# A two-stage fused kernel: first load moved to another issuer as f32, late rows re-laid on every fourth partition and gathered in two transfers, first tiles added singly

## The chip, the cores and the metric

The kernel runs on one core of one Trainium2 chip. The views show five engines of a core, each with its own instructions: TensorE (PE, with PEld its weight loads), VectorE (DVE), ScalarE (ACT), GpSimd (POOL) and SyncE (SP), and 16 DMA engines. The metric is the device time of one execution in microseconds (us), as a median of several runs; the profile of one execution gives a span that is about 1.8 us shorter than that run's time. "PEclk" in a view is the clock granted to TensorE, 1.00 being full. All runs quoted are in the same state ("fast").

Two measures appear below beside the time. One is a view of the profile, copied as it stands. The other is worked out from the single packet records of the DMA engines in the trace; those tables stand in ordinary fences, and I say how each number was formed. Packet times are counted from the same zero as the views.

## The reference, cut to what matters

```python
def phi(x): return np.where(x > 0, x, np.exp(x) - 1.0) + 1.0

# stage 1: linear attention, q, k, v are [8 batches, 8 heads, 576, 64] f32
q_p, k_p = phi(q), phi(k)
kv  = einsum('bhsd,bhse->bhde', k_p, v);  z = sum(k_p, axis=2)
x   = einsum('bhsd,bhde->bhse', q_p, kv) / (einsum('bhsd,bhd->bhs', q_p, z) + 1e-6)
x   = x as [8, 576, 512]                                      # heads side by side

# stage 2: spectral mixing, w_r and w_i are [64 modes, 512, 512] f32
X = rfft(x, axis=1)[:, :64]
Y = X @ (w_r + 1j * w_i), mode by mode                        # complex, 64 of 289 modes kept
y = irfft(Y, n=576, axis=1)
u = x + y
return u + maximum(u @ w_ch, 0.0)                             # [8, 576, 512] f32
```

The weights dominate: 64 modes times 2 times 1 MB is 134 MB, q, k and v are 28 MB, the output is 9.4 MB.

## The kernel before

All loads of q, k, v and weights go out from GpSimd and are cast on the way (f32 in memory, f16 or bf16 on the core: one batch's q is 1.18 MB in memory and 576 KB in the profile's list of DMA issues). The weights stream through a ring of buffers for nearly the whole run. What can be done before the last weight lands is done before: attention rows, the inverse transform of modes 0 to 31 (to 55 for batches 0 and 1), and the products of all modes to 55 with `w_ch`. What is left for after the last weight is a tail: the modes 56 to 63 ("late modes") are transposed, multiplied with `w_ch`, sent to the partitions where the inverse transform wants them, and then 36 tiles of 128 rows are finished in 18 pairs, rectified and stored.

The head. GpSimd issues q, k and v of batch 0; SyncE at the same time issues two small constants:

```python
    nc.sync.dma_start(out=id16, in_=id16_dr.ap())          # 128x128 f16
    nc.sync.dma_start(out=fwd_sb, in_=fwd_dr.ap())         # 160 KB f16
    ...
    def load(b):
        for nm, src in (("q", q), ("k", k), ("v", v)):
            t = sA.tile([128, NHP, NJ * Dh], F16, tag=f"{nm}16", bufs=2, name=f"{nm}16_{b}")
            pin(nc.gpsimd.dma_start(out=t, in_=src[b].rearrange(...)))
            raw[nm, b] = t

    def features(b):                       # phi(x) = min(exp(x), max(x, 0) + 1)
        ...                                # tensor_scalar on raw, tensor_tensor min
```

The last mode. The last weight half comes in two parts, three quarters and one; before it PE is kept busy by six filler matmuls (`keep_warm`), then multiplies in the two parts:

```python
        product(1, wr, range(NDC))
        keep_warm(FILL[kk][0])                              # FILL[63] = (6,)
        product(0, wi, range(3))
        product(0, wi, range(3, NDC))
        nc.vector.tensor_copy(out=YT[:, :, kk, :], in_=y_last)
```

The gather. `last` holds the 128 rows of the late modes (8 modes x real and imaginary x 8 batches), in two planes: Y itself and Y times `w_ch`. `YZ[b]` holds for batch b the rows of modes 32 to 63, twice (partitions 0 to 63 and 64 to 127); rows 48 to 63 of each half are the late ones and come from `last`, by one 32 KB transfer for each batch and half. Two of the sixteen are not needed:

```python
    for b in (2, 3, 0, 1, 4, 5, 6, 7):
        for h in range(1 if b < N_LEAD else 2):
            nc.gpsimd.dma_start(out=YZ[b][64 * h + 48 : 64 * h + 64, :, :], in_=last[b::B, :, :])
```

Tile pairs 0 to 3 (batches 0 and 1) need no gather: they multiply `last` directly. Pair 4 is the first to need it. Tiles 0 and 1 are stored singly (256 KB each), later tiles in pairs (512 KB), all from SyncE:

```python
    store(0, 1)
    relu(0, 1);  rectified(1);  channels(2)
    add_inverse(0, 0, (1,))
    ...                                                     # add tile 1
    store(1, 1)
    channels(3);  rectified(2)
    finish(1)                                               # tiles 2 and 3 as a pair
    ...
```

## Time and profile before

| | before |
|---|---|
| time, median of 3 runs | 429.22 us (429.17 to 429.39) |
| span of the profiled run | 427.4 us |
| DMA load queue, share of the span | 99.0% |
| last weight landed (its DMA's semaphore complete) | about 394.3 us |
| first store issued | 398.08 us |

The page's table of DMA queues (packets, MB, share of 16 engines' span) and the shares by engine of the chain of waits that ended last, for the kernel before:

```profile
q0 software_dynamic: 32256, 82.26, 99.0%
...
DMA 73%; PE 12%; DVE 6%; issue 5%; POOL 1%; ACT 1%; DVEq 0%; POOLq 0%
```

The run is bound by one queue of casting loads that never stops. A change that gives time back must make this queue start sooner, or shorten what comes after its last byte. So two stretches matter.

The windows view of the kernel before: the stretch in us, its length, busy time and instructions of PE, PEld, DVE, ACT and POOL, then PEclk, the DMA share and the GB/s moved. A casting load is counted by its 16-bit bytes (82.26 MB on the load queue, 0.46 MB of it gathers, for about 164 MB in memory), so 205 GB/s of it read 410 GB/s from memory; a store or an f32 load counts in full. The share can exceed 1.

```profile
2.00:3.00 1.00, 0.00 (x0) 0.00 (x0) 0.00 (x0) 0.22 (x2) 1.00 (x3) 1.00 0.66 164
3.00:4.00 1.00, 0.00 (x0) 0.00 (x0) 0.00 (x0) 0.00 (x0) 1.00 (x2) 1.00 0.79 77
9.00:10.00 1.00, 0.00 (x0) 0.00 (x0) 0.00 (x0) 1.00 (x2) 0.00 (x0) 1.00 1.21 205
...
397.00:398.00 1.00, 1.00 (x6) 0.48 (x5) 0.89 (x2) 0.59 (x2) 0.77 (x2) 1.00 0.00 0
399.00:400.00 1.00, 1.00 (x7) 0.49 (x6) 0.40 (x2) 0.85 (x2) 1.00 (x3) 1.00 0.86 297
401.00:402.00 1.00, 1.00 (x6) 0.46 (x6) 1.00 (x1) 0.75 (x3) 1.00 (x3) 1.00 0.47 160
403.00:404.00 1.00, 1.00 (x6) 0.16 (x5) 1.00 (x2) 0.98 (x3) 0.92 (x2) 1.00 0.90 285
405.00:406.00 1.00, 1.00 (x10) 0.26 (x6) 0.97 (x2) 0.77 (x2) 0.00 (x0) 1.00 0.90 307
```

The timeline of the kernel before (start, length, engine, line, operation, number of instructions, and in brackets the idle time before and what ended it), head and tail:

```profile
0.74 0.34 SPq L85 DMA_DIRECT2D id<-ident  x1
1.26 0.90 POOL L164 DMA_DIRECT2D q<-in_q_dram  x1 [0.82 <-POOLq L820]
8.15 2.22 ACT L182 ACTIVATE qe<-q 128x1152 f16<-128x1152 f16 x2 [5.92 <-DMA q<-in_q_dram]
11.05 2.22 ACT L182 ACTIVATE ke<-k 128x1152 f16<-128x1152 f16 x2 [0.68 <-DMA k<-in_k_dram]
...
394.64 0.22 DVE L402 CAST YT<-y_last 128x64 f16<-128x64 f32 x1 [2.69 <-PE y_last L391]
397.23 6.69 POOL L771 DMA_DIRECT2D YZ<-last  x14 [17.79 <-DVE last L765]
398.08 9.41 SPq L671 DMA_DIRECT2D out_dram<-x_main  x8
```

Issuing the first q load takes GpSimd 0.90 us, and q is used only at 8.15 us. The 14 gathers take GpSimd 6.69 us, from 397.23 to 403.9. The cast of `y_last` at 394.64 follows directly on the products of the last weight, so I use it below as the tail's start.

### The profile page before, as it was taken

Reading aid. Unit: us, or ns where it says so; the run is one execution under the profiler, and the core shown is the slowest. Engines: PE = TensorE matmul, PEld = TensorE weight load, DVE = VectorE, ACT = ScalarE, POOL = GpSimd, SP = SyncE. Lnnn points to the kernel's source line nnn. Section 1 sums busy time; section 2 is a strip of 40 time slices with the busy share of each in tenths; the row PEclk is TensorE's granted clock in tenths of the full one; section 3 lists DMA queues with packets and bytes.
Section 4 is the critical chain, followed back from the end, with each engine's and each line's share of the span. In section 5 each row is a group of like instructions: output and inputs, shape, how many; then the busy total and the mean of one; then the engine's idle time right before and its main releaser. Section 6 shows DMA issues by size and latency. Waiting matters only on the chain.

```text
span 427.4 us, 6617 instructions
## 1 busy us (share of the span) xinstructions
PE 285.4 (67%) x2692; PEld 158.9 (37%) x2692; DVE 212.1 (50%) x432; ACT 153.7 (36%) x240; POOL 95.6 (22%) x173
## 2 busy tenths in 40 slices
PE   0357777788119765655333697777788788999991
PEld 0346655564003433333111333433333344374320
DVE  0699998956003755556200433443354344421893
ACT  3588666640102100000000244444353353431781
POOL 4233223212201322112112122122122122010600
PEclk9996666656557755555555569999898899799996
DMA  8999999999999999999999999999999999996698
GB/s 146 207 208 209 209 210 209 211 214 214 218 212 214 213 214 213 215 212 214 213 213 214 213 214 212 214 214 214 214 213 214 214 214 212 213 213 135 211 404 313
DMA packets 35854, 92.46 MB, mean 216 GB/s; under 512 B 3216, under 2 KB 16400, under 8 KB 35824
## 3 DMA queue, kind: packets, MB, share of 16 engines
q0 software_dynamic: 32256, 82.26, 99.0%
q1 hardware_dynamic: 3568, 9.78, 6.0%
q8 instruction: 21, 0.34, 0.3%
q14 instruction: 9, 0.07, 0.0%
HBM read 163.93 MB, written 9.44 MB: 406 GB/s over the span
## 4 chain that ended last, share of the span: by engine, by line
DMA 73%; PE 12%; DVE 6%; issue 5%; POOL 1%; ACT 1%; DVEq 0%; POOLq 0%
DMA wr<-in_moe_w_r_dram 48%; DMA wi<-in_moe_w_i_dram 13%; DMA pick_sb<-row_pick 4%; DMA q<-in_q_dram 4%; DMA k<-in_k_dram 4%; PE P L349 3%; PE acc L616 3%; DVE x L267 2%; PE acc L655 2%; PE z L579 1%; PE zb L606 1%; PE eps L557 1%; PE zb L605 1%; DVE qe L195 1%; ACT ke L182 1%
## 5 line engine op out<-in xcount | busy, mean ns | idle before, releaser
L349 PE MATMUL P<-wi,xt_c 128*32 128x512 bf16 x252 | 37.8, 536 | 39.7 <-DMA wi<-in_moe_w_i_dram 39.7
L360 ACT CAST ys<-P 128x512 f16<-128x512 f32 x31 | 18.2, 586 | 125.3 <-PE P L349 125.3
L110 POOL DMA_DIRECT2D wr<-in_moe_w_r_dram x64 | 34.0, 532 | 124.4 <-PE P L349 102.2
L110 POOL DMA_DIRECT2D wi<-in_moe_w_i_dram x65 | 34.5, 531 | 117.7 <-PE P L349 82.8
L358 DVE CAST ys<-P 128x512 f16<-128x512 f32 x32 | 22.1, 691 | 72.3 <-PE P L349 72.2
L349 PEld LDWEIGHTS <-xt_c 128*32 128x32 bf16 x504 | 28.9, 155 | 76.3 <-issue 65.2
L349 PE MATMUL P<-wr,xt_c 128*32 128x512 bf16 x252 | 37.5, 532 | 23.0 <-DMA wr<-in_moe_w_r_dram 20.8
L538 DVE TENSOR_TENSOR x_main<-ya,x_main 128x512 f32<-128x512 f32 x32 | 22.1, 691 | 39.7 <-PE ya L534 39.6
L557 PE MATMUL eps<-wch,xTw 128*128 128x512 f16 x144 | 41.3, 415 | 0.0
L146 PEld LDWEIGHTS <-qT 64*128 64x128 f16 (+1 forms) x640 | 23.3, 126 | 41.1 <-issue 20.7
L365 PE MATMUL yt<-pick_sb,ys 128*128 128x16 f16 x252 | 16.5, 175 | 25.5 <-DMA pick_sb<-row_pick 15.1
L540 ACT CAST x16w<-x_main 128x512 f16<-128x512 f32 x32 | 19.8, 618 | 34.7 <-DVE x_main L538 34.7
L565 ACT CAST E<-eps 128x512 f16<-128x512 f32 (+1 forms) x40 | 21.3, 543 | 26.6 <-PE eps L557 26.6
L146 PE MATMUL num<-kv,qT 64*128 64x65 f16 (+1 forms) x320 | 13.5, 223 | 22.5 <-ACT kv L242 18.7
L365 PEld LDWEIGHTS <-ys 128*128 128x128 f16 x252 | 12.2, 102 | 40.5 <-issue 17.8
L182 ACT ACTIVATE qe<-q 128x1152 f16<-128x1152 f16 x16 | 17.7, 1155 | 22.7 <-DMA q<-in_q_dram 22.7
L211 PE MATMUL qTp<-id,qe 128*128 128x128 f16 x144 | 16.8, 312 | 12.4 <-DVE qe L195 12.0
L267 DVE TENSOR_TENSOR x<-num,rd 128x512 f16<-128x512 f32 x32 | 22.1, 692 | 1.1
L146 PE MATMUL nw<-kv,qT 64*128 64x65 f16 (+1 forms) x320 | 19.6, 236 | 1.1 <-DVE x_tail L508 0.9
L211 PEld LDWEIGHTS <-qe 128*128 128x128 f16 x144 | 14.7, 147 | 13.2 <-DVE qe L195 12.0
L182 ACT ACTIVATE ke<-k 128x1152 f16<-128x1152 f16 x16 | 17.7, 1155 | 4.9 <-DMA k<-in_k_dram 4.9
L665 ACT ACTIVATE acc<-acc 128x512 f32<-128x512 f32 x34 | 18.1, 581 | 2.3 <-PE acc L616 1.7
(101 smaller groups left out, 451.8 us busy)
## 6 DMA issues: line engine op xcount, KB each, us to landing
wr<-in_moe_w_r_dram POOLq DMA_DIRECT2D x64, 512.0 KB, 18.8
wi<-in_moe_w_i_dram POOLq DMA_DIRECT2D x63, 512.0 KB, 18.9
out_dram<-x_main SPq DMA_DIRECT2D x14, 512.0 KB, 5.8
q<-in_q_dram POOLq DMA_DIRECT2D x8, 576.0 KB, 13.1
k<-in_k_dram POOLq DMA_DIRECT2D x8, 576.0 KB, 14.5
v<-in_v_dram POOLq DMA_DIRECT2D x8, 576.0 KB, 16.7
out_dram<-x_main SPq DMA_DIRECT2D x4, 256.0 KB, 3.6
out_dram<-x_tail SPq DMA_DIRECT2D x2, 512.0 KB, 5.3
```

Source lines behind the costliest of these rows:

```text
L110: tc.keep_in_program_order(nc.gpsimd.dma_start(out=w[:, dcs], in_=rows_of[:, dcs, :]))
L146: mm = nc.tensor.matmul(num[hpo][orow, c0 : c0 + 65], qT[rows, hpp, h2, cols], kv_sb[rows, hpp, h2, :])
L182: pin(nc.scalar.activation(out=ev[:, c], in_=heads(nm, b)[:, c], func=AF.Exp))
L211: nc.tensor.transpose(qT_ps[:, j].rearrange("p t r -> p (t r)"), phi["q", b][:, hpp, j].rearrange("p o d -> p (o d)"), id16,)
L267: nc.vector.tensor_tensor(out=dst.rearrange("p (o c d) -> p o c d", o=2, c=4), in0=nv[:, :, :, 0:64], in1=rden.unsqueeze(3).broadcast_to([ ...
L349: nc.tensor.matmul(P[dc * 32 : dc * 32 + 32, :], xt_cols(dc, t, kk), w[:, dc, :], start=(t == 1), stop=(t == 0), tile_position=(0, dc * 32),)
L358: fixed(nc.vector.tensor_copy(out=st, in_=P))
L365: nc.tensor.matmul(yt_ps[:, ec, kk % 8, :], st[:, ec * 128 : ec * 128 + 128], pick_sb)
L538: pin(nc.vector.tensor_tensor(out=x, in0=acc, in1=x, op=ALU.add))
L540: pin(nc.scalar.copy(out=x16w[t], in_=x))
L557: nc.tensor.matmul(e_ps, xT[:, c, :], wch16[:, c, :], start=(c == 0), stop=(c == NDC - 1))
L565: pin(nc.scalar.copy(out=dst, in_=e_ps[:, cols]))
```

## The change: intent and core of the diff

Three parts, each meant for one of the two stretches.

1. **Head.** Batch 0's q is loaded as f32 without a cast, in two halves, from SyncE, whose first issue is at 0.74 us, so that GpSimd can begin with k. The constants follow q in SyncE's queue. VectorE and ScalarE read q as f32 for this batch.
2. **Layout and gather.** The late rows of each half lie on partitions 0, 4, 8, ... 60 (and 64, 68, ...) instead of 48 to 63 and 112 to 127. All eight batches lie in one tile, so that the whole of `last` goes over in two 256 KB transfers, one from SyncE and one from GpSimd.
3. **Singles.** Tiles 2 and 3, like 0 and 1, are added and stored one by one. Two batches late in the tail are stored as 1 MB instead of twice 512 KB.

```diff
-    nc.sync.dma_start(out=id16, in_=id16_dr.ap())
-    nc.sync.dma_start(out=fwd_sb, in_=fwd_dr.ap())
 ...
     def load(b):
         for nm, src in (("q", q), ("k", k), ("v", v)):
+            if (nm, b) == ("q", 0):
+                for c in range(2):
+                    t = sA.tile([128, 2, NJ * Dh], F32, tag="x16", bufs=2, name=f"q32_{c}")
+                    pin(nc.sync.dma_start(out=t, in_=rows_in[:, c::2, :]))
+                    raw[nm, b, c] = t
+                pin(nc.sync.dma_start(out=id16, in_=id16_dr.ap()))
+                pin(nc.sync.dma_start(out=fwd_sb, in_=fwd_dr.ap()))
+                continue
 ...   # row selection (sel) and the tiles of transposed modes (YT -> YE_T, YL, Y8) follow the new layout
-    YZ = [sW.tile([128, 2, D], F16, tag="YZ", bufs=B, name=f"YZ{b}") for b in range(B)]
+    YZ_all = sW.tile([128, B, 2, D], F16, tag="YZ", bufs=1, name="YZ_all")
+    YZ = [YZ_all[:, b] for b in range(B)]
 ...   # 1 MB stores
+    QUADS = (5, 6)
+        if t0 < B * NJJ and t0 // NJJ in QUADS:
+            if t0 % NJJ:
+                store(t0 - 2, NJJ)
+            return
 ...   # the eviction of the transposed late modes is split between ScalarE and VectorE
-    for b in (2, 3, 0, 1, 4, 5, 6, 7):
-        for h in range(1 if b < N_LEAD else 2):
-            nc.gpsimd.dma_start(out=YZ[b][64 * h + 48 : 64 * h + 64, :, :], in_=last[b::B, :, :])
+    for h, eng in enumerate((nc.sync, nc.gpsimd)):
+        eng.dma_start(
+            out=YZ_all[64 * h : 64 * h + 64 : NF // NL].rearrange("r b z d -> r b (z d)"),
+            in_=last.rearrange("p z d -> p (z d)"),
+        )
 ...   # singles
-    channels(3)
-    rectified(2)
-    finish(1)
+    rectified(2)
+    for i in range(2):
+        add_inverse(1, 0, (i,))
+        add_one(1, i)
+    channels(3)
```

More of the change, by code (lines that the diff above doesn't have):

```diff
@@ L161, in load, with heads, flat @@
         for nm, src in (("q", q), ("k", k), ("v", v)):
-            t = sA.tile([128, NHP, NJ * Dh], F16, tag=f"{nm}16", bufs=2, name=f"{nm}16_{b}")
-            pin(
-                nc.gpsimd.dma_start(
-                    out=t,
-                    in_=src[b].rearrange("h s d -> (h s) d").rearrange(
-                        "(hp r j) d -> r hp (j d)", r=128, j=NJ
-                    ),
-                )
-            )
-            raw[nm, b] = t
-    def heads(nm, b):
-        return raw[nm, b].rearrange("p (o c) (j d) -> p c o j d", o=2, d=Dh)
+            rows_in = src[b].rearrange("h s d -> (h s) d").rearrange(
+                "(hp r j) d -> r hp (j d)", r=128, j=NJ
+            )
[7 more added lines that the diff above has]
+                continue
+            t = sA.tile([128, NHP, NJ * Dh], F16, tag=f"{nm}16", bufs=2, name=f"{nm}16_{b}")
+            pin(nc.gpsimd.dma_start(out=t, in_=rows_in))
+            raw[nm, b] = t
+    def heads(nm, b, c):
+        if (nm, b) == ("q", 0):
+            return raw[nm, b, c].rearrange("p o (j d) -> p o j d", d=Dh)
+        return raw[nm, b].rearrange("p (o c) (j d) -> p c o j d", o=2, d=Dh)[:, c]
+    def flat(nm, b):
+        tiles = [raw[nm, b, c] for c in range(2)] if (nm, b) == ("q", 0) else [raw[nm, b]]
+        return [t.rearrange("p a f -> p (a f)") for t in tiles]
     def exps(b):
@@ L181, in exps @@
             for c in range(2):
-                pin(nc.scalar.activation(out=ev[:, c], in_=heads(nm, b)[:, c], func=AF.Exp))
+                pin(nc.scalar.activation(out=ev[:, c], in_=heads(nm, b, c), func=AF.Exp))
     def features(b):
         for nm in ("q", "k"):
-            rf = raw[nm, b].rearrange("p a f -> p (a f)")
             ev = phi[nm, b].rearrange("p c j o d -> p c o j d")
-            pin(
-                nc.vector.tensor_scalar(
-                    out=rf, in0=rf, scalar1=0.0, scalar2=1.0, op0=ALU.max, op1=ALU.add
+            for rf in flat(nm, b):
+                pin(
+                    nc.vector.tensor_scalar(
+                        out=rf, in0=rf, scalar1=0.0, scalar2=1.0, op0=ALU.max, op1=ALU.add
+                    )
                 )
-            )
             for c in range(2):
@@ L195, in features @@
                     nc.vector.tensor_tensor(
-                        out=ev[:, c], in0=ev[:, c], in1=heads(nm, b)[:, c], op=ALU.min
+                        out=ev[:, c], in0=ev[:, c], in1=heads(nm, b, c), op=ALU.min
                     )
@@ L252, in form_x @@
             x16s[b] = (
-                sA.tile([128, NJJ, D], F16, tag="x16", bufs=2, name=f"x16_{b}"),
+                sA.tile([128, 2 * NJ * Dh * 2], F16, tag="x16", bufs=2, name=f"x16_{b}")[
+                    :, 0 : NJJ * D
+                ].rearrange("p (j d) -> p j d", j=NJJ),
                 sA.tile([128, D], F16, tag="x16t", bufs=2, name=f"x16t_{b}"),
@@ L401, in last_mode @@
         product(0, wi, range(3, NDC))
-        nc.vector.tensor_copy(out=YT[:, :, kk, :], in_=y_last)
+        nc.vector.tensor_copy(out=Y8[:, :, NL - 1, :], in_=y_last)
     while pending:
@@ L422 @@
     lead_sb = [ystage.tile([128, S], F16, name=f"lead{b}_sb") for b in range(N_LEAD)]
-    sel = ystage.tile([128, 1 + N_LEAD, 128], F16, name="row_sel")
+    sel = ystage.tile([128, D], F16, tag="ystage", bufs=2, name="row_sel")[
+        :, 0 : (1 + N_LEAD) * 128
+    ].rearrange("p (n c) -> p n c", c=128)
     nc.sync.dma_start(out=inv_sb, in_=inv_dr.ap())
@@ L426, with mode_rows @@
     for h in range(2):
-        nc.vector.tensor_copy(out=sel[:, 0, h * 64 : h * 64 + 64], in_=id16[:, 2 * NF : 128])
+        for g in range(NF // NL):
+            r0 = 2 * NF + 2 * NL * ((g - 1) % (NF // NL))
+            nc.vector.tensor_copy(
+                out=sel[:, 0, h * 64 + g : h * 64 + 64 : NF // NL], in_=id16[:, r0 : r0 + 2 * NL]
+            )
     for b in range(N_LEAD):
         nc.vector.tensor_copy(out=sel[:, 1 + b, b:128:B], in_=id16[:, 2 * NE : 128])
-    YT = ystage.tile([128, NDC, NM, 2 * B], F16, name="YT")
-    nc.vector.memset(YT[:, :, NE:NM, :], 0.0)
+    YE_T = ystage.tile([128, NDC, NF, 2 * B], F16, name="YE_T")
+    YL = ystage.tile([128, NDC, 2 * NL, NF // NL, B], F16, name="YL")
+    Y8 = ystage.tile([128, NDC, NL, 2 * B], F16, name="Y8")
+    nc.vector.memset(YL[:, :, :, 0, :], 0.0)
+    def mode_rows(ps):
+        return ps.rearrange("p c m (t b) -> p c (m t) b", b=B)
     yt_ps = None
@@ L442, in mode @@
         if kk == NM - 2:
-            pin(nc.vector.tensor_copy(out=YT[:, :, NE : NM - 1, :], in_=yt_ps[:, :, 0 : NL - 1, :]))
+            pin(nc.vector.tensor_copy(out=Y8[:, :, 0 : NL - 1, :], in_=yt_ps[:, :, 0 : NL - 1, :]))
         elif kk % 8 == 7:
-            ins = nc.vector.tensor_copy(out=YT[:, :, kk - 7 : kk + 1, :], in_=yt_ps)
-            if kk >= NF:
-                pin(ins)
+            if kk < NF:
+                nc.vector.tensor_copy(out=YE_T[:, :, kk - 7 : kk + 1, :], in_=yt_ps)
+            else:
+                g = (kk - NF) // NL + 1
+                pin(nc.vector.tensor_copy(out=YL[:, :, :, g, :], in_=mode_rows(yt_ps)))
     for kk in range(n_early):
@@ L519, in early_rows @@
         for ec in range(NDC):
-            yt = YT[:, ec, 0:NF, :].rearrange("p m (t b) -> p (m t) b", b=B)[:, :, b]
+            yt = YE_T[:, ec].rearrange("p m (t b) -> p (m t) b", b=B)[:, :, b]
             pin(nc.tensor.transpose(y_ps[:r, ec, :], yt, id16))
@@ L575, in form_z @@
         for ec in range(NDC):
-            yt = YT[:, ec, NF:NM, :].rearrange("p m (t b) -> p (m t) b", b=B)[:, :, b]
+            yt = YL[:, ec].rearrange("p k g b -> p (k g) b")[:, :, b]
             for h in range(2):
@@ L589, in form_y @@
         for ec in range(NDC):
-            yt = YT[:, ec, NF:NM, :].rearrange("p m (t b) -> p (m t) b", b=B)[:, :, b]
+            yt = YL[:, ec].rearrange("p k g b -> p (k g) b")[:, :, b]
             for h in range(2):
@@ L742 @@
                 work.append(lambda n=n: channels(n))
-    last_ps.append(psW.tile([128, D], F32, tag="P", bufs=2, name="zl1"))
-    y_ps = psW.tile([128, NDC, 128], F16, tag="P", bufs=2, name="ypl")
-    y0_ps = psW.tile([128, NDC, 8, 2 * B], F32, tag="yt", bufs=1, name="y0l")
-    rows = [YT[:, ec, NE:NM, :].rearrange("p m n -> p (m n)") for ec in range(NDC)]
+    z1_ps = psW.tile([128, NDC, 8, 2 * B], F32, tag="yt", bufs=1, name="z1l")
+    y_ps = [
+        psW.tile([128, NDC, 128], F16, tag="P", bufs=2, name=f"ypl{h}")[:, 0 : NDC // 2] for h in range(2)
+    ]
+    y0 = psW.tile([128, D], F32, tag="P", bufs=2, name="y0l")
+    last_ps.append(z1_ps.rearrange("p c m n -> p (c m n)"))
+    rows = [Y8[:, ec].rearrange("p m n -> p (m n)") for ec in range(NDC)]
+    hw = D // 2
+    COLS = [slice(h * hw, h * hw + hw) for h in range(2)]
     for ec in range(NDC):
-        pin(nc.tensor.transpose(y_ps[:, ec, :], rows[ec], id16))
-    pin(nc.scalar.copy(out=last[:, 0, :], in_=y_ps.rearrange("p c r -> p (c r)")))
-    hw = D // 2
+        pin(nc.tensor.transpose(y_ps[ec // 2][:, ec % 2, :], rows[ec], id16))
+    pin(nc.scalar.copy(out=last[:, 0, COLS[0]], in_=y_ps[0].rearrange("p c r -> p (c r)")))
+    pin(nc.vector.tensor_copy(out=last[:, 0, COLS[1]], in_=y_ps[1].rearrange("p c r -> p (c r)")))
     for h in range(2):
-        cols = slice(h * hw, h * hw + hw)
         for ec in range(NDC):
@@ L757 @@
                 nc.tensor.matmul(
-                    last_ps[h][:, 0:hw], rows[ec], wch16[:, ec, cols],
+                    last_ps[h][:, 0:hw], rows[ec], wch16[:, ec, COLS[h]],
                     start=(ec == 0), stop=(ec == NDC - 1),
@@ L761 @@
             )
-        if h == 0:
-            pin(nc.scalar.copy(out=last[:, 1, cols], in_=last_ps[h][:, 0:hw]))
-        else:
-            pin(nc.vector.tensor_copy(out=last[:, 1, cols], in_=last_ps[h][:, 0:hw]))
-    y0 = y0_ps.rearrange("p c m n -> p (c m n)")
+        pin(nc.scalar.copy(out=last[:, 1, COLS[h]], in_=last_ps[h][:, 0:hw]))
     pin(nc.tensor.matmul(y0, lead_sb[0][:, rows_of(0)], last[:, 0, :]))
     pin(nc.vector.tensor_tensor(out=x_of(0), in0=y0, in1=x_of(0), op=ALU.add))
-    for b in (2, 3, 0, 1, 4, 5, 6, 7):
-        for h in range(1 if b < N_LEAD else 2):
-            nc.gpsimd.dma_start(out=YZ[b][64 * h + 48 : 64 * h + 64, :, :], in_=last[b::B, :, :])
+    for h, eng in enumerate((nc.sync, nc.gpsimd)):
+        eng.dma_start(
+            out=YZ_all[64 * h : 64 * h + 64 : NF // NL].rearrange("r b z d -> r b (z d)"),
+            in_=last.rearrange("p z d -> p (z d)"),
+        )
     psW.release()
@@ L779, in relu, with add_one @@
         on_bank(n, {i}, nc.scalar.activation(out=a, in_=a, func=AF.Relu))
+    def add_one(n: int, i: int):
+        t = pairs[n][i]
+        on_bank(n, {i}, nc.vector.tensor_tensor(out=x_of(t), in0=accs[n][:, i], in1=x_of(t), op=ALU.add))
+        store(t, 1)
     add_inverse(0, 1)
@@ L792 @@
     add_inverse(0, 0, (1,))
-    on_bank(0, {1}, nc.vector.tensor_tensor(out=x_of(1), in0=accs[0][:, 1], in1=x_of(1), op=ALU.add))
-    store(1, 1)
+    add_one(0, 1)
+    rectified(2)
+    for i in range(2):
+        add_inverse(1, 0, (i,))
+        add_one(1, i)
     channels(3)
-    rectified(2)
-    finish(1)
     rectified(3)
```

## The prediction

> **What bounds the kernel now.** DMA, nearly end to end. The DMA-queue table gives the load queue 99.0% of the span. In the stretch table the 16 engines move 205 to 217 GB/s (the f16 side of casting loads; twice that is read) from 8 us to 390 us without a gap. The chain of waits is 73% DMA. Only two stretches fall short and can give time back:
>
> - Head. Before 2 us almost nothing moves; at 2-3 us only two constants (164 GB/s, share 0.66, full being about 1.2), at 3-4 us 77 GB/s, then 167-190 until 7 us. GpSimd issues the first q load at 1.26 us; it lands 6.9 us later.
> - Tail. The last weight lands at 394.3 us, the first store issues at 398.1. DMA moves 189, 238, 341, 341 GB/s in the two-microsecond steps from 398, then 382 to 422 until 424. Compute ends at 420.1, the stores about 425.1, the span 427.4: stores, not PE (2.45 us for two pairs) or VectorE (1.18 us a pair), set the end once backed up. 9.44 MB at 406 GB/s is 23.2 us.
>
> **Middle.** Everything between (more small row-selection copies, strided evictions of late modes, a few PE instructions reordered) sits under loads that never run dry. Worth about 0.
>
> **Head.** q of batch 0 (1.18 MB f32) goes out from SyncE, which issued its first DMA at 0.74 us, with bytes from about 1.9 us[...]. The constants move behind it. I count 7.25 us of full DMA work before 10 us now; starting fully at 1.9 would give 8.1. Estimated gain 0.9 us, carried unchanged through the saturated stream. VectorE pays for f32: two tensor_scalars of about 0.75 for one of 0.76, two minima near 1.36 for 0.75[...]. These 2 us fall where VectorE sat idle 8.9 us: free.
>
> **Tail.** Fourteen 32 KB gathers cost GpSimd 6.7 us of issue (397.2 to 403.9) and write 16 neighbouring partitions. [...] Two 256 KB transfers issued near 396.7 should land by 400.5, before tile pair 4 needs them (401). Splitting tiles 2 and 3 brings 256 KB stores at about 400.1 and 400.8 instead of 512 KB at 401.0. Split evictions gain about 0.2. Store backlog should form about 1.1 us earlier. The two 1 MB stores: about 0.
>
> **Sum.** 0.9 + 1.1 = 2.0 us, all on the critical path: 427.2 us, range 425.7 to 428.5. Chances: faster by over 2% 0.01, within 2% 0.985, slower 0.005.
>
> **What would show it.** Head: q landing by 6 us, DMA share above 1.1 from 3 us, k landing a microsecond before 11.05, last weight at 393.4; if that still lands at 394.3, the head gain was swallowed. Middle: 213 GB/s unbroken. Tail: gathers landed by 400.5, over 380 GB/s at 402-406, first store to DMA end about 26 us against 27.
>
> **What would make it wrong.** SyncE's first store slips behind the gather in its queue; the gather is slow and PE waits at pair 4; SyncE's q delays k0, so VectorE, 97% busy from 30 to 60 us, starves loads; reordered PE work frees weight buffers too late. More gain if neighbouring-partition writes held back stores more than the 0.65 us that the missing rate at 402-406 suggests.

The sum: 0.9 us for the head and 1.1 for the tail, 2.0 together, so 427.2 us. The tail's 1.1 is the prediction's own estimate.

## More of the kernel before

In the head DMA runs at 77 GB/s from 3 to 4 us, where 205 is the level it reaches later. In the tail it moves nothing from 397 to 398 us and then 160 to 307 GB/s in every other microsecond until 406, where stores alone reach 400 to 416.

## The result, and the profile after

The changed kernel took 427.62 us (6 runs, 427.21 to 428.15) against 429.2 us (6 runs, 428.86 to 429.39) of the kernel before. The ratio is 0.9965, with a 95% interval of 0.9952 to 0.9978: within 2%, and about 1.6 us faster. Ratios in this document are the mean time of one kernel's fast runs over that of the other's of the same rounds, so not quite the ratio of the medians that I quote. The prediction of 427.2 us, and its range, hold. The profiled runs' spans are 427.4 us before and 425.4 after.

The same lines for the changed kernel. Queues and chain of waits:

```profile
q0 software_dynamic: 31360, 81.48, 98.3%
...
DMA 69%; PE 12%; issue 8%; DVE 7%; ACT 2%; POOL 1%; DVEq 0%; POOLq 0%; ACTq 0%
```

The windows view:

```profile
2.00:3.00 1.00, 0.00 (x0) 0.00 (x0) 0.00 (x0) 0.22 (x2) 1.00 (x3) 1.00 0.61 120
3.00:4.00 1.00, 0.00 (x0) 0.00 (x0) 0.00 (x0) 0.00 (x0) 1.00 (x2) 1.00 1.03 408
9.00:10.00 1.00, 0.45 (x5) 0.46 (x6) 1.00 (x2) 0.31 (x1) 0.00 (x0) 1.00 1.21 205
...
397.00:398.00 1.00, 1.00 (x6) 0.42 (x5) 0.91 (x2) 1.00 (x4) 0.00 (x0) 1.00 1.00 297
399.00:400.00 1.00, 1.00 (x6) 0.26 (x4) 0.66 (x2) 0.79 (x2) 0.00 (x0) 1.00 1.07 377
401.00:402.00 1.00, 1.00 (x7) 0.26 (x6) 1.00 (x2) 0.74 (x3) 0.00 (x0) 1.00 0.91 361
403.00:404.00 1.00, 1.00 (x10) 0.42 (x8) 1.00 (x2) 0.75 (x3) 0.00 (x0) 1.00 0.99 401
```

The timeline of the changed kernel, head and tail:

```profile
0.74 0.94 SPq L166 DMA_DIRECT2D q<-in_q_dram  x2
4.78 1.16 ACT L190 ACTIVATE qe<-q 128x1152 f16<-128x1152 f32 x1 [2.55 <-DMA q<-in_q_dram]
6.27 1.16 ACT L190 ACTIVATE qe<-q 128x1152 f16<-128x1152 f32 x1 [0.33 <-DMA q<-in_q_dram]
9.69 2.22 ACT L190 ACTIVATE ke<-k 128x1152 f16<-128x1152 f16 x2 [2.26 <-DMA k<-in_k_dram]
...
393.35 0.22 DVE L412 CAST Y<-y_last 128x64 f16<-128x64 f32 x1 [3.08 <-PE y_last L401]
395.34 0.64 SPq L801 DMA_DIRECT2D YZ_all<-last  x1
395.62 0.56 POOL L801 DMA_DIRECT2D YZ_all<-last  x1 [16.54 <-ACT last L797]
396.68 9.15 SPq L696 DMA_DIRECT2D out_dram<-x_main  x9
```

What the reader is to see: q is used at 4.78 and 6.27 us instead of 8.15, and k at 9.69 instead of 11.05. The whole tail is 1.3 us earlier from its start (393.35 for 394.64). The gather costs GpSimd 0.56 us instead of 6.69. From 403 us on the stores run at 401 GB/s, where they had 285 to 307 in every other microsecond.

Between the two stretches nothing moved in the rate: from 200 to 210 us, to take one stretch, both kernels move 212 GB/s at share 1.06, although TensorE's granted clock is 0.50 there in both.

To split the gain between head and tail, I worked these points out of the packet records of each trace: when 3 MB and 160 MB of source data had been moved by loads, when the last load packet ended, when the cast of `y_last` started, and when 99% of all later packets (stores and gather, without those of 4 bytes) had ended. Not a view of the profile:

```
us             3 MB    160 MB  last load  y_last cast  99% of later   cast to
               moved   moved   packet     starts       packets ended  99%
before         10.96   382.42  393.98     394.64       425.19         30.6
changed        10.26   381.78  392.65     393.35       422.68         29.3
difference      0.70     0.64    1.33       1.29         2.51          1.2
```

So 0.7 us was won by the time 3 MB had been moved, and 0.64 of it was still there at 160 MB. The loads' end is another 0.7 us earlier; that part arises in the last eleven microseconds, where the queue drains. It is not a matter of this pair alone: from 160 MB to the last load packet it took 10.8 to 10.9 us in seven of the eight traces with q first on SyncE (11.8 in the eighth, `c_split`), 11.3 to 11.9 in the five traces without the head, and 11.1 with the constants ahead of q. Why it goes with the head stays open. After the cast the tail is 1.2 us shorter. The spans differ by 2.0 us and not 2.5, since the last one percent of packets and what follows it took 2.8 us in the changed run and 2.3 before.

### The profile page after: what moved, and what is told of

Same layout as the page of the kernel before. It is cut to its first block, busy times and chain, and to the rows that moved or that the text cites. A ratio compares the mean times of both kernels' runs of the same rounds, so it can differ in the third digit from the quotient of the medians.

```text
span 425.4 us, 6619 instructions
## 1 busy us (share of the span) xinstructions
PE 285.7 (67%) x2692; PEld 160.0 (38%) x2692; DVE 214.5 (50%) x440; ACT 154.1 (36%) x241; POOL 88.3 (21%) x159
## 4 chain that ended last, share of the span: by engine, by line
DMA 69%; PE 12%; issue 8%; DVE 7%; ACT 2%; POOL 1%; DVEq 0%; POOLq 0%; ACTq 0%
DMA wi<-in_moe_w_i_dram 51%; DMA wr<-in_moe_w_r_dram 9%; DMA k<-in_k_dram 9%; PE acc L641 3%; PE P L359 2%; DVE x L277 2%; PE acc L680 2%; ACT ke L190 1%; PE z L604 1%; DVE ke L203 1%; DVE k L197 1%; PE zb L631 1%; PE zb L630 1%; DVE qe L203 1%; PE yb L626 1%
## 5 line engine op out<-in xcount | busy, mean ns | idle before, releaser
L144 PEld LDWEIGHTS <-qT 64*128 64x128 f16 (+1 forms) x640 | 25.3, 126 | 41.6 <-issue 21.3
L190 ACT ACTIVATE qe<-q 128x1152 f16<-128x1152 f16 (+1 forms) x16 | 17.8, 1157 | 17.8 <-DMA q<-in_q_dram 17.8
L219 PE MATMUL qTp<-id,qe 128*128 128x128 f16 x144 | 16.7, 309 | 10.1 <-DVE qe L203 9.5
L144 PE MATMUL nw<-kv,qT 64*128 64x65 f16 (+1 forms) x320 | 22.1, 236 | 1.6 <-DVE x_tail L533 1.0
```

What stands on the lines that cost most here:

```text
L144: mm = nc.tensor.matmul(num[hpo][orow, c0 : c0 + 65], qT[rows, hpp, h2, cols], kv_sb[rows, hpp, h2, :])
L190: pin(nc.scalar.activation(out=ev[:, c], in_=heads(nm, b, c), func=AF.Exp))
L219: nc.tensor.transpose(qT_ps[:, j].rearrange("p t r -> p (t r)"), phi["q", b][:, hpp, j].rearrange("p o d -> p (o d)"), id16,)
```

## The experiments

Twelve runs were made (the changed kernel twice more and ten edited ones), each beside fresh runs of the kernel before on the same chip. Kernels are compared only within the same rounds. All results were correct. My theory at the start was: the head gives its gain by starting the stream earlier; the tail gives its gain by earlier and freer stores (singles, and a gather that neither trickles nor goes to neighbouring partitions). Rivals: the head's gain is swallowed by the stream, the singles or the gather alone carry the tail, the spread over the partitions alone does it, or the order of the constants matters.

### Which part brings what (first call; the kernel before took 429.52 us, 428.75 to 431.94)

**Head only.** The kernel before with the head of the change and nothing else:

```diff
-    nc.sync.dma_start(out=id16, in_=id16_dr.ap())
-    nc.sync.dma_start(out=fwd_sb, in_=fwd_dr.ap())
...
+            if (nm, b) == ("q", 0):        # as in the change: two f32 halves and both constants on SyncE
```

> The kernel before with the head change alone (q of batch 0 as f32 from SyncE, constants behind it). Theory (the head gain is carried whole through the saturated load stream): last weight lands at 393.0 us instead of 394.3, time 1.3 us lower, about 427.9. Rival (the earlier stream only lengthens the store backlog at the end, since stores set the end): last weight at 393.0 but time less than 0.5 us lower.

Measured: 428.94 us (428.33 to 429.41), ratio 0.9981 (0.9961 to 1.0000). The gain is 0.6 us: less than the 1.3 us of the theory, and just above the rival's limit of 0.5. 3 MB had been moved at 10.20 us and 160 MB at 381.73, as in the changed kernel; to this point the head's gain goes through the stream whole. The last load packet ended 1.4 us earlier than before (392.55 for 393.98), but in this profiled run the last weight landed 0.9 us after its last packet (393.44), where the kernel before took 0.3 (394.27). The section on the last quarter below comes back to this.

**Two transfers, old layout.** Fourteen gathers merged into two, still to 16 neighbouring partitions of each half:

```diff
-    for b in (2, 3, 0, 1, 4, 5, 6, 7):
-        for h in range(1 if b < N_LEAD else 2):
-            nc.gpsimd.dma_start(out=YZ[b][64 * h + 48 : 64 * h + 64, :, :], in_=last[b::B, :, :])
+    for h, eng in enumerate((nc.sync, nc.gpsimd)):
+        eng.dma_start(out=YZ_all[64 * h + 48 : 64 * h + 64].rearrange("r b z d -> r b (z d)"),
+                      in_=last.rearrange("p z d -> p (z d)"))
```

In the expectation, theory A is that the spread over the partitions decides and theory B that the number of transfers does. A's words for it, here and in the next run, named a cause that no run shows, and are cut.

> The kernel before with its fourteen gathers merged into two (one from SyncE, one from GpSimd), still onto 16 neighbouring partitions. Theory A [...]: the two gathers take over 6 us to land, DMA moves under 250 GB/s while they run, PE or the stores wait; time at or above that of before. Theory B (the number of transfers matters, GpSimd's 6.7 us of issue): they land in under 4.5 us and the time falls 0.5 us or more.

Measured: 430.84 us (430.31 to 431.97), ratio 1.0024 (1.0003 to 1.0045): slower than the kernel before. Its profile says why. The view of one tile's transfers (time from issue to landing), the view of waits inside the tail (total us, times, longest), and the windows view of this kernel:

```profile
DMA to landing us min/median/max: 4.5/5.2/5.9
...
PE acc L617 <- DMA YZ_all<-last: 1.6, 1, 1.6
...
401.00:402.00 1.00, 0.87 (x4) 0.24 (x3) 1.00 (x2) 0.64 (x2) 0.00 (x0) 1.00 1.14 168
402.00:403.00 1.00, 0.03 (x1) 0.00 (x0) 0.54 (x1) 0.58 (x1) 0.00 (x0) 1.00 0.87 188
```

The transfers land 4.5 and 5.9 us after their issue, PE waits 1.6 us for the second at tile pair 4 and does almost nothing from 402 to 403 us. DMA is full meanwhile (share 1.14) but moves 168 GB/s: its packets are slow, not few. This profiled run also had TensorE at half clock in two stretches (370 to 376 us and 404 to 407), so I don't take the size of the loss from it; but all six timed runs lie above 430.3, and the ratio puts the loss at 1.0 us.

**New layout, fourteen transfers.** The new layout with the old gathers and without head, singles and 1 MB stores:

```diff
     for b in (2, 3, 0, 1, 4, 5, 6, 7):
         for h in range(1 if b < N_LEAD else 2):
-            nc.gpsimd.dma_start(out=YZ[b][64 * h + 48 : 64 * h + 64, :, :], in_=last[b::B, :, :])
+            nc.gpsimd.dma_start(out=YZ_all[64 * h : 64 * h + 64 : NF // NL, b], in_=last[b::B, :, :])
```

> The new row layout (every fourth partition) with fourteen transfers from GpSimd, no head change, no single tiles, no 1 MB stores. Theory A [...]: DMA moves more than 350 GB/s at the four microseconds in which before moved 341, gain 0.4 us or more. Theory B (number of transfers): no gain, within 0.2 us of before.

Measured: 429.34 us (428.89 to 431.78), ratio 0.9999 (0.9974 to 1.0024): nothing. The windows view of this kernel shows the same holes as that of the kernel before:

```profile
401.00:402.00 1.00, 1.00 (x6) 0.35 (x4) 1.00 (x2) 0.75 (x3) 1.00 (x3) 1.00 0.52 152
403.00:404.00 1.00, 1.00 (x6) 0.15 (x4) 1.00 (x2) 0.98 (x3) 0.50 (x2) 1.00 0.88 277
```

**New layout, two transfers.** As the last, with the change's two gathers:

```diff
-            nc.gpsimd.dma_start(out=YZ_all[64 * h : 64 * h + 64 : NF // NL, b], in_=last[b::B, :, :])
+    for h, eng in enumerate((nc.sync, nc.gpsimd)):
+        eng.dma_start(out=YZ_all[64 * h : 64 * h + 64 : NF // NL].rearrange("r b z d -> r b (z d)"),
+                      in_=last.rearrange("p z d -> p (z d)"))
```

> The new row layout with two transfers, no head change, no single tiles, no 1 MB stores. Both theories: gain 0.4 to 0.8 us over before, as this is the gather part of the change entire. If the gain is under 0.2 us, the single tiles made the tail gain and the gather nothing.

Measured: 427.95 us (427.63 to 430.85), ratio 0.9971 (0.9944 to 0.9997): 1.6 us faster than the kernel before. The time to landing and the windows view of this kernel:

```profile
DMA to landing us min/median/max: 3.2/3.5/3.9
...
399.00:400.00 1.00, 1.00 (x6) 0.57 (x5) 0.40 (x2) 0.96 (x2) 0.00 (x0) 1.00 1.02 303
403.00:404.00 1.00, 1.00 (x6) 0.15 (x4) 1.00 (x2) 0.97 (x3) 0.00 (x0) 1.00 1.00 401
```

The stores have 401 GB/s at 403 us, like the changed kernel and without its singles. The packet records put these four side by side (mean time of one packet of the gathers that GpSimd issued; start of the cast to 99% of later packets, now to two places). The SyncE half of a merged gather goes in packets of 2048 bytes on the queue of the stores, and I can't tell the two apart. The 32.61 us fell in the run with TensorE partly at half clock:

```
                     transfers  partitions      gather packet         cast to 99%
before               14         16 neighbours   2048 B, 104 ns        30.56 us
new layout, 14       14         every fourth    2048 B, 115 ns        30.44
old layout, 2         2         16 neighbours   4096 B, 510 ns        32.61
new layout, 2         2         every fourth    4096 B, 200 ns        29.45
```

Neither half of the change does anything good alone. Spreading the rows changes nothing as long as the transfers come one at a time; sending them all at once is worse than before on neighbours, and 1.1 us better on every fourth partition. Both new-layout kernels also carry the split evictions and the reordered work of the change; with fourteen transfers these bring at most the 0.1 us by which the first two rows differ.

The same records give the time in which the 16 DMA engines had nothing to move between the cast and the 99% point (that stretch less the packet time over 16): 4.7 us before, 4.5 with the new layout and fourteen transfers, 4.6 with two on the old layout, and 3.3 with two on the new one and in the changed kernel. The packets themselves took 25.9 to 26.2 us, but 28.0 with two transfers on the old layout.

### The whole, and its parts taken out (second call; the kernel before took 428.94 us, 428.23 to 430.12)

**The changed kernel again**, unedited.

> The changed kernel again, as the yardstick of this call. 1.6 to 2.0 us under before (median of six was 1.6, the profiled run 2.0). Last weight's product copied out 1.3 us earlier than before's 394.6, from there to the end of the span 32.1 us (before 32.8).

Measured: 427.55 us (426.97 to 427.86), ratio 0.9962 (0.9946 to 0.9978): the gain of 1.4 us repeats.

**Without the head.** The changed kernel with the loads of the kernel before:

```diff
-            if (nm, b) == ("q", 0):        # two f32 halves and both constants on SyncE
+            pin(nc.gpsimd.dma_start(out=t, in_=...))   # q as f16 from GpSimd, constants first on SyncE
```

> The change without its head part. Theory (head and tail gains add): 0.7 to 1.5 us under before, last copy at 394.6 as in before, from there to the end 32.1 us. Rival (the tail gain needs the earlier stream): within 0.3 us of before.

Measured: 428.13 us (427.56 to 428.29), ratio 0.9976 (0.9958 to 0.9993). The head is worth 0.58 us by this difference and 0.58 by the first call's (429.52 less 428.94). The tail alone is worth 0.8 us here; the new layout with two transfers had 1.6 in the first call. Medians of a few runs do not fix it closer than that, and the packet records, with 29.35 us from cast to 99% here against 30.56, give 1.2.

**Without singles and 1 MB stores.**

```diff
-    QUADS = (5, 6)
+    QUADS = ()
...
-    rectified(2)
-    for i in range(2):
-        add_inverse(1, 0, (i,))
-        add_one(1, i)
     channels(3)
+    rectified(2)
+    finish(1)
     rectified(3)
```

> The change without the single stores of tiles 2 and 3 and without the 1 MB stores; head and two spread gathers stay. Theory from the runs so far (the gather is the whole tail gain, as the gather itself already keeps DMA busy while the early stores are missing): within 0.2 us of the changed kernel, 32.1 us from last copy to the end. Rival, as predicted (early single stores are worth 0.5 us or more): 0.5 us slower than the changed kernel.

Measured: 427.79 us (427.46 to 428.09), ratio 0.9969 (0.9953 to 0.9985). That is 0.24 us above the changed kernel of the same call, within the scatter of either; from cast to 99% of packets it took 29.48 us for 29.33. The singles and 1 MB stores together are worth 0.1 to 0.2 us at most.

**Constants ahead of q.** One edit, the order of four issues on SyncE:

```diff
             if (nm, b) == ("q", 0):
+                pin(nc.sync.dma_start(out=id16, in_=id16_dr.ap()))
+                pin(nc.sync.dma_start(out=fwd_sb, in_=fwd_dr.ap()))
                 for c in range(2):
                     ...
-                pin(nc.sync.dma_start(out=id16, in_=id16_dr.ap()))
-                pin(nc.sync.dma_start(out=fwd_sb, in_=fwd_dr.ap()))
```

The rival calls the constants small slow packets. In the trace of the kernel before, their 256-byte packets took 17 ns in the mean and their 1280-byte packets 74 ns (138 for the first 23, begun before 2.5 us); in that of the changed kernel q's 2304-byte packets took 93 ns from 3 us on.

> The changed kernel with the two constants ahead of q on SyncE, as they stood before. Theory (the head gain is the time in which DMA had nothing to move, whoever goes first): k of batch 0 used by ScalarE within 0.3 us of the changed kernel's 9.69 us, time within 0.3 us of it. Rival (moving the constants behind q is half of the head gain, as they are small slow packets at the very start): k used 0.5 us later or more, time 0.5 us higher.

Measured: 428.20 us (427.76 to 430.97), ratio 0.9990 (0.9965 to 1.0014): 0.65 us above the changed kernel, which is all that the head had brought. The timeline of this kernel:

```profile
6.61 1.16 ACT L190 ACTIVATE qe<-q 128x1152 f16<-128x1152 f32 x1 [4.38 <-DMA q<-in_q_dram]
10.32 1.16 ACT L190 ACTIVATE qe<-q 128x1152 f16<-128x1152 f32 x1 [2.54 <-DMA q<-in_q_dram]
11.39 2.20 ACT L190 ACTIVATE ke<-k 128x1152 f16<-128x1152 f16 x2
```

The second half of q comes 4 us later than in the changed kernel (10.32 for 6.27), far more than the 192 KB of constants take to move (1.4 us in the kernel before, from 1.71 to 3.10 us). The packet records show what is different. In the changed kernel q's first 24 packets (2304 bytes each), begun between 1.8 and 2.5 us, took 519 ns in the mean, those from 3 us on 93 ns, and k's packets began only at 5.4 us, though GpSimd had issued k at 1.25: SyncE's q had the DMA engines to itself. With the constants ahead, the constants' small packets fill 1.7 to 3.1 us, q's packets begin at 2.8 and still take 282 ns from 3 to 3.5 us, and from 4.2 us on k's packets share the engines with q until 9.8. 3 MB had been moved at 10.78 us, against 10.1 to 10.3 in the eight traces with q first and 10.7 to 11.0 in the five without the head. So here q from SyncE was worth something only when it was first. Why the DMA engines let one queue run alone, and then not, these runs do not show.

### Two attempts to gain more (third and fourth call)

**The changed kernel once more** (third call; the kernel before took 429.01 us, 428.24 to 430.06).

> The changed kernel as yardstick of this call: 1.4 to 1.6 us under before.

Measured: 427.28 us (426.99 to 427.92), ratio 0.9955 (0.9943 to 0.9967).

**The gather split by plane**, the first half sent as soon as the transposed modes are ready, while DMA has nothing to do (0 GB/s from 393.0 to 396.5 us in the first trace of the changed kernel):

```diff
+    def gather(z):
+        for h, eng in enumerate((nc.sync, nc.gpsimd)):
+            pin(eng.dma_start(out=YZ_all[64 * h : 64 * h + 64 : NF // NL, :, z, :], in_=last[:, z, :]))
+
+    gather(0)                              # before the products with w_ch
...
-    for h, eng in enumerate((nc.sync, nc.gpsimd)):     # the two whole gathers
-        ...
+    gather(1)
```

> The changed kernel with each gather cut in two: the half of the late rows that is ready first (the transposed modes, about 0.9 us before the other half) is sent at once, while DMA has nothing to move. Theory (stores set the end, so gather bytes moved before the first store are time saved; 512 KB took about 1.8 us of DMA at 290 GB/s): 0.4 to 0.9 us under the changed kernel. Rival (more and smaller packets, 1 KB runs, and two more issues on SyncE and GpSimd ahead of the first store eat it): within 0.2 us of the changed kernel or slower.

Measured: 427.77 us (427.14 to 429.58), ratio 0.9970 (0.9954 to 0.9987): not faster than the changed kernel's 427.28. Its profiled run had TensorE at half clock from 394.9 to 398.3 us, just in the work that leads to the first stores, and was the slowest of its six, so its trace can't say where the expected gain went in the others. That stays open.

**When PE comes to the last quarter of the last weight.** The changed kernel's runs fall in two groups, near 427.2 and near 428.0. A trace of each group differs at one place. The timeline of two runs of the same changed kernel, first the one of 427.21 us, then one of 427.84 us of the third call:

```profile
392.38 0.94 PE L401 MATMUL y_last<-xt_c,wi 128*128 128x16 bf16 x16
```

```profile
392.23 0.53 PE L401 MATMUL y_last<-xt_c,wi 128*128 128x16 bf16 x12
393.49 0.29 PE L401 MATMUL y_last<-xt_c,wi 128*128 128x16 bf16 x4 [0.73 <-DMA wi<-in_moe_w_i_dram]
```

In the first PE waited for the last quarter for little more than 0.1 us; in the second it waited 0.73 us and lost about 0.6 us against the first. The theory before the fourth call was that PE loses this if it comes to the last quarter before its data, and that one filler matmul more would avoid it. (That PE came before its data was read from packet times counted 0.24 us too late; on the zero of the views the last packet of the second run ended at 392.55, before PE's wait began.) The fourth call tried seven fillers, and three, which let PE come early (the kernel before took 429.36 us, 428.42 to 430.09).

```diff
-    FILL = {61: (2, 2, 1), 62: (5, 3, 3), 63: (6,)}
+    FILL = {61: (2, 2, 1), 62: (5, 3, 3), 63: (7,)}     # and 63: (3,) in the other
```

> The changed kernel with seven filler products instead of six ahead of the last weight half, so that TensorE comes to the last quarter 0.22 us later. Its times fall in two groups, about 427.1 and 427.9[...]. Theory (a TensorE that has to wait there loses 0.6 us over one that comes just late): most runs in the 427.1 to 427.4 group, median 0.2 to 0.4 us under the changed kernel's 427.3 to 427.6. Rival (the groups come from elsewhere): both groups as before, median 0 to 0.2 us higher.

> Three filler products instead of six: TensorE comes to the last quarter 0.65 us earlier and has to wait in every run. Theory: all runs in the slow group, 427.8 to 428.2, and the profile shows the wait of about 1.4 us with the resume 0.6 us or more after the last packet. Rival: times as the changed kernel's or better, with the resume 0.1 to 0.2 us after the last packet.

Measured: seven fillers 427.84 us (426.93 to 428.04; five runs, of which three are in the slower group), ratio 0.9957 (0.9945 to 0.9970); three fillers 428.46 us (427.09 to 429.13), ratio 0.9980 (0.9966 to 0.9994). Three fillers gave four slow runs of five. The fifth, with 427.09, has a trace in which TensorE was at half clock from 368.7 to 375.5 us, so that PE came late after all. The times look like half a confirmation, but seven fillers did not remove the slower group, and a trace contradicts the theory. It is the profiled run of the changed kernel in the second call, 427.83 us, so of the slower group. Its timeline, later than in the two runs above:

```profile
392.97 0.94 PE L401 MATMUL y_last<-xt_c,wi 128*128 128x16 bf16 x16
```

The last load packet of this run had ended at 392.62. The weight loads for the first twelve of these matmuls were done at 393.37, long after it, and the next one still had to wait for the DMA until 393.62. What is late is the landing, that is the completion of the DMA's semaphore, which PE waits for. Worked out from the semaphore times in the traces: in eleven of the fourteen kept traces the last weight landed 0.26 to 0.33 us after its last packet, in the other three (the changed kernel in the second and third call, and the head alone) 0.89 to 0.96 us after. Where PE had to wait, it went on 0.04 to 0.05 us after the landing, both early and late. The five traces of the changed kernel and its two filler variants fit: the two with the late landing have 427.83 and 427.84 us, the three others 427.09 to 427.23. So the late landing, and not the moment at which PE comes, goes with the slower group. Why a landing is late stays open; all three are among the eight traces with q first on SyncE, too few to conclude from. The slow runs with three fillers have no trace.

No experiment beat the changed kernel.

## Why the prediction was right, point by point

**The sum was right.** Predicted 427.2 us and a gain of 2.0; measured 427.62, and in the later calls 427.55 and 427.28, with gains of 1.6, 1.4 and 1.7 us by the medians and 2.0 by the profiled spans. That it came so near is partly luck: the head brought less than forecast, and the tail's share came from another part of the change than the one it was credited to. The bound was read right: one load queue at 99.0% of the span, with a head and a tail as the only places to gain.

**Head: right in kind, 0.9 us predicted, 0.6 to 0.7 measured.** 3 MB had been moved 0.7 us earlier, the time is 0.58 us better with the head in either kernel, and the stream carried the gain to 160 MB. (The last load packet came even 1.3 us earlier, which the prediction did not foresee and the times do not show in full; landings that are 0.6 us late, as described above, took part of it back in three of the eight traces with q first.) The predicted signs: "q landing by 6 us" came nearly so (its halves used at 4.78 and 6.27 us), "k landing a microsecond before 11.05" came at 9.69, "last weight at 393.4" came at 393.0. The sign "DMA share above 1.1 from 3 us" was mis-set: the share was 1.03 to 1.05 at 408 to 410 GB/s; the casting loads, from 9 to 10 us, took a share of 1.21 for the same source bytes (205 GB/s of f16 from 410 of f32). The missing 0.2 to 0.3 us fits the estimate "starting fully at 1.9": the first packets came at 1.8 us but took 519 ns in the mean, and full rate was reached at 3 us only (120 GB/s from 2 to 3).

SyncE's first bytes came about 1.1 us after its issue at 0.74 in the changed kernel (first q packet at 1.81), and GpSimd's q about 1.7 us after its issue at 1.26 in the kernel before (2.91).

**Head: the order of the constants was not costed.** The prediction says "The constants move behind it" and gives this no value. The medians put it at 0.65 us, as much as the whole head. Moving q to SyncE with the constants ahead gives nothing: 428.20 us, where the same kernel without the head took 428.13.

**VectorE's price: right.** The prediction put 0.75 us on each of the two tensor_scalars with f32 and 1.36 on each of the two minima. Measured were 0.76 us for each tensor_scalar (128x1152, f32) and up to 1351 ns for a minimum with f32, against a median of 758 for the group of 16 minima of that size, 14 of them on f16 alone. The trace of the kernel before would have given the minimum, too: its tensor_tensors with f32 took 692 ns for 128x512 and 1222 for 128x1024, and a line through the two gives 1.35 us for 128x1152 (an estimate). And it was free, as predicted: VectorE idled before it (5.2 us before the two tensor_scalars), and PE's first transposes still began 2.5 us earlier (9.55 for 12.01).

**Middle: right.** Worth nothing, and the rate unchanged.

**Tail: the size was right (1.1 us predicted, 1.2 by the packet records, 0.8 to 1.6 by the medians), the parts were not.** This is the step that failed. The prediction put the gain together from "Splitting tiles 2 and 3 brings 256 KB stores at about 400.1 and 400.8 instead of 512 KB at 401.0", from split evictions, and from earlier issue; it gave the gather a share only through slow writes on neighbouring partitions, and for the rest asked only that it not be late. The runs show the reverse: the gather alone (new layout, two transfers) gives 1.1 us by the packet records (30.56 to 29.45), and without the singles and the 1 MB stores the changed kernel misses only 0.15 us of its packet time and 0.24 us of its median.

The split evictions, for which the prediction allowed 0.2 us, are part of the kernel with the new layout and fourteen transfers, which gained 0.1 us by its packets and nothing by its times.

The mechanism, as the windows show it: in the kernel before, the fourteen gathers are issued every 0.48 us (6.69 us over 14) from 397.2 to 403.9, so they leave DMA half empty while stores are scarce (160 GB/s at 401 to 402 us) and take bytes when stores are plentiful (285 and 307 GB/s at 403 and 405). In the changed kernel the two transfers fill the time from 396.6 to 398.9, when hardly any store is ready, and after that stores alone run at 401. The idle time of the DMA engines after the cast fell from 4.7 to 3.3 us with this, at equal packet time.

**The neighbouring partitions: they count, but not where the prediction put it.** The prediction took writes to 16 neighbouring partitions to be slow and saw in that a possible reason for the missing rate in the kernel before (0.65 us by its estimate, from 341 GB/s at 402-406 against 406 later). The runs show no such loss there: with fourteen transfers one after another a packet took 104 ns on neighbours and 115 ns on the spread rows. Only when all the bytes are sent at once does the spread tell: 510 ns for a packet of 4096 bytes on neighbours, 200 ns on every fourth. Why neighbours are slower then is not shown; no run separates one cause from another. So the layout is not worth anything by itself; it is what makes the two large transfers possible, which on the old layout cost 1.3 us.

"Gathers landed by 400.5" was right (398.5 and 399.5), as was "first store to DMA end about 26 us against 27": from the first store's issue to 99% of packets it is 26.0 us (396.68 to 422.68) against 27.1 (398.08 to 425.19). "Over 380 GB/s at 402-406" was right too (401 to 410).

## What to carry to other kernels

When a stream of loads is full from end to end, look at the first bytes and at what follows the last: here a load that came first in its issuer's queue was worth 0.6 us, and the same load behind two small constants nothing. Look too at small transfers in the middle of a store phase: here fourteen of 32 KB, sent instead as two of 256 KB while DMA was idle, saved 1.1 us by the packet records with the destination on every fourth partition; on neighbouring ones the merged transfers lost 1.0 us by the ratio. Test the parts of such a change one by one and also together: here neither the layout nor the merging gained alone, and a prediction that gets the sum right can still credit the wrong part.
